# A long convolution's filter spectrum, kept in SBUF for the first group

## The chip, the core and the metric

The kernel runs on one core of a Trainium2 chip. The metric is the device time of one execution in microseconds, the median of several runs. A profile of one execution is at hand beside the times; its engines are PE (TensorE), DVE (VectorE), ACT (ScalarE), POOL (GpSimd) and SP (SyncE, which here only issues transfers).

## What is computed

Two stages, in float32 at the borders. The first is a causal convolution of x (8 batches, 5696 tokens, 128 channels) with a filter h (5696 tokens, 128 channels), by Fourier transforms of twice the length; the second mixes the tokens of its result with two 5696 x 5696 matrices and ends with a small channel product.

```python
L = 2 * S                                  # S = 5696
Y = np.fft.rfft(x, n=L, axis=1) * np.fft.rfft(h, n=L, axis=0)[None]
x = np.fft.irfft(Y, n=L, axis=1)[:, :S, :]
theta = x @ w_theta
zr, zi = x * np.cos(theta), x * np.sin(theta)
u = x + einsum('ts,bsd->btd', w_tok_r, zr) + einsum('ts,bsd->btd', w_tok_i, zi)
out = u + np.maximum(u @ w_ch, 0)
```

## The kernel before

**Groups.** x is worked on in eight groups: four pairs of batches (bp) by two halves of the channels (dh, 64 channels each). The two batches of a pair share one pass as the two halves of the 128 partitions. The transform of length 11392 is split as 178 x 64, and only 90 of the 178 rows (K1 = 90) are needed. A group goes through four stages.

- Stage a (`stage_a`, L241): 16 chunks of four matmuls (L250), each evicted by ACT (L259) or DVE (L257) into a tile `a` of 2 x 90 x 64 float16 columns. The pool that holds `a` has one buffer. The first transform of h goes through the same function and takes that buffer; group 0 has another one (`a_0`), and group 1 takes the buffer of h when h no longer needs it.
- Stage b (`stage_b`, L407): 12 chunks of eight rows (the last has two). 32 small matmuls (`f2`, L262, L270) finish the transform of a chunk, ACT evicts them as `xs` (L426), and DVE multiplies by the spectrum of h and writes `uv_t` (L428; the narrow last chunk L433). A complex product needs the spectrum twice: straight, and with real and imaginary halves swapped. The two halves lie on partitions 0 to 63 and 64 to 127, so a swap moves data across partitions. A tile `hs` (four buffers, `LEAD` = 4) holds both forms of one chunk, and one instruction multiplies by both.
- Stage c (`stage_c`, L439): 16 chunks of sixteen matmuls (L448, L449), evicted by DVE (L455) or ACT (L453) as `g`.
- Stage d (`stage_d`, L473): the last matmuls (L484) and the store of the convolved values.

Stage a of group g+1 is woven into stage c of group g, and stage d of group g into stage b of group g+1.

**The spectrum of h.** `h_chunk` (L351) runs the twelve chunks of `f2` on h, evicts each (DVE L357 or ACT L359) into `hst`, a region of `uv_t` that the products overwrite later, and after every third chunk issues two stores to `hf_hbm` (L364; real and imaginary halves, 384 KB each, eight in all). `hf_hbm` has room for both forms on 128 rows. For group 0 (`first`) two loads per chunk read it back (L416 straight, L417 swapped, 128 KB each, 24 in all). `swap_rows` (L397) then makes the swapped form in HBM by four copies from HBM to HBM (L402, 768 KB each), so that the other seven groups read a chunk with one load (L419).

**Order.** The code around group 0 is: twelve `h_chunk`s with two chunks of stage a between them, the first four chunks' loads, the rest of stage a of group 0, then stage b of group 0, in whose last three chunks three chunks of stage a of group 1 are woven (L541 and L542), then `swap_rows`, then stage c of group 0 woven with the rest of stage a of group 1 and with the making of the tables for stage d (`e_table`, L384). DVE, ACT and POOL keep the order of the code (`manual_schedule`, up to L789). PE and SP do not: a planner orders them by the code's order among what it holds to be ready. Transfers issued by SP go into one hardware queue over the 16 DMA engines; POOL issues the loads of x into another (128-byte pieces, converted to float16 on the way). Nothing on SP is issued before the stores of h.

**The clock.** PE's clock is granted in full or in half. `idle` (L239) and the `warm` matmuls (L276) compute nothing that is used; they keep PE busy.

Lines to have at hand:

```python
        for ri in range(2 if c % 3 == 2 else 0):
            nc.sync.dma_start(hf_hbm[c - 2:c + 1, :, :64, ri, :]..., hst[...])
...
            if first:
                nc.sync.dma_start(hs[:64], hf_hbm[c, dh, :64])
                nc.sync.dma_start(hs[64:], hf_hbm[c, dh, :64, ::-1, :])
            else:
                nc.sync.dma_start(hs, hf_hbm[c, dh])
```

Of the kernel before, what the change touches and what calls it, by code (L numbers as in the profile page):

```python
# [14 lines left out]
mult = mybir.AluOpType.mult  # L15
# [7 lines left out]
def kernel(  # L23
# [10 lines left out]
    nc = tc.nc  # L34
    B, S, D = x.shape
    assert D == 128
    P = 128
# [42 lines left out]
    CK = 8  # L80
    HD = D // 2
# [5 lines left out]
    CHK = [(c0, min(CK, K1 - c0)) for c0 in range(0, K1, CK)]  # L87
    NCK = len(CHK)
# [9 lines left out]
    hf_hbm = nc.dram_tensor("hf_hbm", (NCK, 2, P, 2, HD * CK), F16, kind="Internal").ap()  # L98
# [5 lines left out]
    def psum():  # L104
        return fp.tile([P, 2, 512], F32, tag="ps", name="ps")
# [18 lines left out]
    u_t, v_t = uv_t[:, :UVW + P], uv_t[:, UVW:]  # L124
# [111 lines left out]
    def idle(ps, n, of, m):  # L236

        for i in range(n):
            nc.tensor.matmul(ps[:, i % 2, 512 - m:], of[:, :P], of[:, P:P + m], start=True, stop=True)  # L239

    def stage_a(lhs, by_dve=(), a_=None, spare=None):  # L241

        st = {}

        def chunk(q):
            if q == 0:
                st["a"] = fa.tile([P, 2 * K1, HD], F16, tag="a", name="a_") if a_ is None else a_
            ps = psum()
            for i in range(4):
                nc.tensor.matmul(ps[:, i // 2, (i % 2) * 2 * K1:(i % 2 + 1) * 2 * K1], lhs(q + i), f1_t[:NB],  # L250
                                 start=True, stop=True)
            if spare is not None:
                idle(ps, *spare)
            a_out = st["a"][:, :, q:q + 4].rearrange("p k (a q) -> p k a q", a=2)
            a_in = ps[:, :, :4 * K1].rearrange("p a (q k) -> p k a q", q=2)
            if q // 4 in by_dve:
                nc.vector.tensor_copy(a_out, a_in)  # L257
            else:
                nc.scalar.activation(a_out, a_in, AF.Copy)  # L259
        return [lambda q=q: chunk(q) for q in range(0, HD, 4)], st  # L260

    def f2(a_st, c, warm=WARM):  # L262

        c0, ck = CHK[c]
        ps = psum()
        for j in range(ck):
            for ri in range(2):
                for e in range(2):
                    rows = slice(64 * e, 64 * e + 64)
                    nc.tensor.matmul(ps[:, e, j * HD:(j + 1) * HD],  # L270
                                     w_t2[rows, c0 + j, N2 * (1 - ri):N2 * (3 - ri)],
                                     a_st["a"][rows, ri * K1 + c0 + j, :],
                                     start=(ri == 0), stop=(ri == 1))
        if c == NCK - 1:
            for n in range(warm):
                nc.tensor.matmul(ps[:, n % 2, ck * HD:ck * HD + 384], w_t2[:, 2, :P],  # L276
                                 w_t2[:, 0:2, :].rearrange("p k n -> p (k n)"), start=True, stop=True)
        return ps[:, :, :ck * HD].rearrange("p e (k d) -> p e d k", k=ck)
# [8 lines left out]

    for f in load_x(0):
        f()
    hst = [t[:, :6 * D * CK].rearrange("p (c h d k) -> p c h d k", c=6, h=2, k=CK) for t in (u_t, v_t)]  # L290
    nc.gpsimd.memset(uv_t[:, 2 * UVW:], 0.0)
    k_d = s1.tile([P, 2 * NP + 2 * ND], F32, tag="k_r", name="k_r")
    for at, step, n, base in ((0, 2, NP, 1), (NP, 2, NP, 1), (2 * NP, 2, N2 // 2, 0),
# [40 lines left out]
    def h_copy(d0):  # L334
# [5 lines left out]
    steps, a_h = stage_a(lambda q: h16[:NB].rearrange("p h n d -> p (h n) d")[:, :, q], (1, 3, 5, 9),  # L340
                         spare=(2, pad, 512 - 4 * K1))
    for n, f in enumerate(steps):
# [5 lines left out]
            w2_sine, w2_cosine = w_round(2)  # L348
        f()

    def h_chunk(c):  # L351
        c0, ck = CHK[c]
        ps = f2(a_h, c, 0)
        h_ = hst[c // 6][:, c % 6]
        dst = h_[:, :, :, :ck]
        if c in (0, 2, 5, 7, 10):
            nc.vector.tensor_scalar(dst, ps, 16.0 / NF, None, op0=mult)  # L357
        else:
            nc.scalar.activation(dst, ps, AF.Copy, scale=16.0 / NF)  # L359
        for cc, j in ((0, 0), (NCK - 1, CHK[-1][1] - 1)):  # L360
            if c == cc:
                nc.vector.tensor_scalar(dst[:, :, :, j], dst[:, :, :, j], 0.5, None, op0=mult)
        for ri in range(2 if c % 3 == 2 else 0):
            nc.sync.dma_start(  # L364
                hf_hbm[c - 2:c + 1, :, :64, ri, :].rearrange("c h p n -> p (c h) n"),
                hst[c // 6][64 * ri:64 * ri + 64, c % 6 - 2:c % 6 + 1].rearrange("p c h d k -> p (c h) (d k)"))

    r_u = fc.tile([P, P], F16)
    r_v = fc.tile([P, RC], F16)
# [25 lines left out]
        return curves  # L395

    def swap_rows():  # L397
        for c0 in range(0, NCK, NCK // 2):
            for ri in range(2):
                dst, src = (hf_hbm[c0:c0 + NCK // 2, :, r0:r0 + 64, r, :].rearrange("c h p n -> (c h) p n")  # L400
                            for r0, r in ((64, ri), (0, 1 - ri)))
                nc.sync.dma_start(dst, src)  # L402

# [3 lines left out]
    def stage_b(a_st, dh, warm=WARM, first=False):  # L407

        hs_of = {}

        def load(c):
            if c >= NCK:
                return
            hs = hs_of[c] = fh.tile([P, 2, HD * CK], F16, tag="hs", name="hs")
            if first:
                nc.sync.dma_start(hs[:64], hf_hbm[c, dh, :64])  # L416
                nc.sync.dma_start(hs[64:], hf_hbm[c, dh, :64, ::-1, :])  # L417
            else:
                nc.sync.dma_start(hs, hf_hbm[c, dh])  # L419

        def chunk(c):
            c0, ck = CHK[c]
            hv = hs_of[c].rearrange("p r (d k) -> p r d k", k=CK)
            ps = f2(a_st, c, warm)
            xs = fs.tile([P, 2, HD, CK], F16, tag="xs", name="xs")
            nc.scalar.activation(xs[:, :, :, :ck], ps, AF.Copy)  # L426
            if ck == CK:
                nc.vector.tensor_tensor(  # L428
                    uv[:, :, :, c0:c0 + ck],
                    xs.rearrange("p e d k -> p e (d k)").unsqueeze(1).to_broadcast([P, 2, 2, HD * CK]),  # L430
                    hv.rearrange("p r d k -> p r (d k)").unsqueeze(2).to_broadcast([P, 2, 2, HD * CK]), op=mult)
            for r in range(2 if ck < CK else 0):
                nc.vector.tensor_tensor(  # L433
                    uv[:, 2 * r:2 * r + 2, :, c0:c0 + ck], xs[:, :, :, :ck],
                    hv[:, r:r + 1, :, :ck].to_broadcast([P, 2, HD, ck]), op=mult)
            load(c + LEAD)
        return [lambda c=c: load(c) for c in range(LEAD)], [lambda c=c: chunk(c) for c in range(NCK)]

    def stage_c(st, last):  # L439
# [65 lines left out]
    def front(g, by_dve=(), a_=None, spare=None):  # L505
        if g >= len(groups):
            return [], [], []
        bp, dh = groups[g]
        x16 = x16s[g].rearrange("p b n d -> p (b n) d")
        steps, a_st = stage_a(lambda q: x16[:NB, :, q], by_dve, a_, spare)  # L510
        return (steps, *stage_b(a_st, dh, WARM if g else WARM // 2, g == 0))

    a0, load0, b0 = front(0, (1, 3, 5, 8, 11, 13), a_0, (1, w_t2[:, 2:5].rearrange("p k n -> p (k n)"), 512 - 4 * K1))
    rr = []
    r_rest = [lambda: rr.extend([r_table(0, r_u), r_table(1, r_v)]), lambda: rr[0](), lambda: rr[1]()]
    h_chunk(0)
    w2_sine()
    w_rest(1)
    h_chunk(1)
    w2_cosine()  # L520
    for c in range(2, NCK):
        if c == 5:
            w_rest(2)
        h_chunk(c)
        if c in (9, 10):
            a0.pop(0)()
# [6 lines left out]
    fronts = {1: front(1)}  # L533
    curves = e_table(0)
    for n, f in enumerate(b0):
        f()
        if n == 5:
            curves()
        if n % 2:
            idle(psum(), 1, w_t2[:, 2:6].rearrange("p k n -> p (k n)"), 512)  # L540
        if n > 8:  # L541
            fronts[1][0].pop(0)()  # L542
    setup.close()
    fg = pool("fft_g", 1, conv, side="right")

# [560 lines left out]
    for i, (k, p, tt, j0, s0, nj) in enumerate(stretches):  # L1106
# [22 lines left out]
        a, nxt = nxt, None if i == 1 else prepare(i + 1, not woven)  # L1129
# [15 lines left out]
        if tt is None:  # L1145
# [24 lines left out]
            if end_of_pair:  # L1170
# [5 lines left out]
                c, c0 = c_last  # L1176
# [161 lines left out]
```

## Time and profile before

| what | value |
|---|---|
| median of 3 runs | 2052.54 us (2051.28 to 2053.35) |
| the profiled execution | 2052.18 us, span 2050.4 us |
| mean granted PE clock | 0.987 |
| PE busy, DVE busy, ACT busy, POOL busy | 96%, 75%, 31%, 47% of the span |
| stores of h to HBM (L364) | 8, issued from 30.7 to 44.4 us |
| loads of h for group 0 (L416, L417) | 24, issued from 44.4 to 67.7 us |
| products of group 0 (L428, L433) | from 54.7 to 70.7 us |
| stage c of group 0 | from 70.4 to about 91 us |

How to read it: a row of instruction groups gives line, engine, operation, the tile written and the tiles read, shapes, count, then busy time in all and the mean of one in ns, then how long the engine was idle before them and what ended that. A line of the time line gives start, duration (of all merged instructions), engine and line, and in brackets the idle time before the first one with its releaser. Times count from the span's start. A line of the stretches gives the length, then busy time and instruction count of PE, PE's weight loads, DVE, ACT and POOL, the granted clock, the DMA engines' share and GB/s.

### The profile page before, as it was taken

What the parts mean: (1) busy time and instruction counts of PE and PEld (TensorE: products, weight loads), DVE (VectorE), ACT (ScalarE), POOL (GpSimd) and SP (SyncE); (2) the same over time, 40 slices, a digit from 0 to 9 for tenths busy, and PEclk for the clock granted to TensorE, in tenths of its full rate; (3) what the DMA queues carried; (4) which work ended last, traced back from release to release, by engine and by line L of the source; (5) the groups of instructions that cost most, each with busy time, mean ns of one, the idle gap of its engine ahead of it and who ended that gap; (6) DMA issues with size and microseconds to landing.
All of it is one profiled execution on the core that took longest, in us unless ns stands there. A gap on an engine that the chain in (4) does not pass through costs nothing.

```text
span 2050.4 us, 42565 instructions
## 1 busy us (share of the span) xinstructions
PE 1959.6 (96%) x16205; PEld 1086.2 (53%) x16381; DVE 1538.9 (75%) x2806; ACT 639.9 (31%) x936; POOL 965.2 (47%) x1769
## 2 busy tenths in 40 slices
PE   7799899799999999999999998999999999999998
PEld 5688888654444444444444443444444444444444
DVE  7787777657788888787867667867777686777767
ACT  6788777872232333333300000011111111111111
POOL 8323312384354545454566454453544535354450
PEclk9899999999999999999999999999999999999999
DMA  9999996999899998999999799797887969788793
GB/s 151 187 180 159 146 171 204 238 293 179 163 179 176 170 180 159 179 173 177 170 168 159 119 251 217 107 152 131 150 145 132 155 124 153 131 150 146 131 156 85
DMA packets 510158, 338.21 MB, mean 165 GB/s; under 512 B 184136, under 2 KB 461256, under 8 KB 509864
## 3 DMA queue, kind: packets, MB, share of 16 engines
q0 software_dynamic: 322368, 157.47, 61.0%
q1 hardware_dynamic: 181600, 166.48, 27.8%
q10 hardware_dynamic: 5984, 11.54, 1.6%
q8 instruction: 128, 2.10, 0.4%
q14 instruction: 78, 0.63, 0.1%
HBM read 379.54 MB, written 95.63 MB: 232 GB/s over the span
## 4 chain that ended last, share of the span: by engine, by line
PE 66%; DVE 3%; DMA 2%; issue 1%; POOL 0%; ACT 0%; DVEq 0%; ACTq 0%; SPq 0%
PE m L1275 62%; DMA b<-z_hbm 1%; DVE c L1282 1%; DVE b L831 1%; PE v L977 1%; PE utp L970 1%; PE m L1279 1%; DVE wt L890 1%; PE theta_ps L560 0%; PE tpz L918 0%; PE m L1162 0%; PE m L1196 0%; POOL ring L676 0%; DMA c<-cp_hbm 0%; DMA wl<-in_moe_w_tok_i_dram 0%
## 5 line engine op out<-in xcount | busy, mean ns | idle before, releaser
L676 POOL DMA_DIRECT2D ring<-in_moe_w_tok_i_dram x720 | 387.9, 546 | 657.7 <-DVE wt L890 576.9
L890 DVE STREAM_TRANSPOSE wt<-ring 128x384 f32<-128x384 f32 (+2 forms) x720 | 360.5, 527 | 127.7 <-PE m L1275 77.7
L676 POOL DMA_DIRECT2D ring<-in_moe_w_tok_r_dram x720 | 386.2, 547 | 142.4 <-DVE wt L890 82.4
L1275 PE MATMUL m<-b,wt 128*128 128x512 bf16 x1605 | 386.6, 380 | 3.7 <-DVE wt L890 1.7
L1275 PEld LDWEIGHTS <-wt 128*128 128x128 bf16 x1804 | 176.3, 98 | 219.5 <-DVE wt L890 7.4
L1282 DVE TENSOR_TENSOR c<-c,m 128x512 f32<-128x512 f32 x412 | 266.8, 674 | 0.4 <-PE m L1275 0.4
L972 ACT ACTIVATE ring<-utp 128x512 bf16<-128x512 bf16 x85 | 50.8, 597 | 582.1 <-PE utp L970 582.1
L428 DVE TENSOR_TENSOR uv_t<-xs,hs 128x2048 f16<-128x2048 f16 x88 | 104.4, 1224 | 29.9 <-ACT xs L426 18.2
L448 PE MATMUL ps<-r_u,uv_t 128*128 128x128 f16 x1024 | 116.5, 219 | 4.7 <-ACT cos L588 1.3
L1196 PE MATMUL m<-b,wt 128*128 128x512 bf16 x471 | 110.3, 379 | 7.6 <-DMA b<-z_hbm 4.2
L967 ACT ACTIVATE ub<-c 128x512 bf16<-128x512 f32 x88 | 55.1, 628 | 192.1 <-DVE c L1237 113.5
L449 PE MATMUL ps<-r_v,uv_t 128*128 128x100 f16 x1024 | 114.1, 207 | 0.5
L153 POOL DMA_DIRECT2D x<-in_x_dram x128 | 97.9, 771 | 22.2 <-POOL x L151 14.9
L426 ACT ACTIVATE xs<-ps 128x1024 f16<-128x1024 f32 x96 | 90.8, 972 | 42.4 <-PE ps L270 21.9
L449 PEld LDWEIGHTS <-uv_t 128*128 128x128 f16 x1024 | 99.9, 98 | 7.1 <-issue 5.7
L448 PEld LDWEIGHTS <-uv_t 128*128 128x128 f16 x1024 | 100.0, 98 | 1.1 <-DVE uv_t L433 0.4
L1196 PEld LDWEIGHTS <-wt 128*128 128x128 bf16 x528 | 50.4, 98 | 65.1 <-issue 8.4
L562 ACT ACTIVATE red<-theta_ps,magic 128x512 f32<-128x512 f32 (+1 forms) x46 | 31.6, 687 | 153.1 <-PE theta_ps L560 80.4
L270 PEld LDWEIGHTS <-w_t 64*128 64x128 f16 x3240 | 59.4, 100 | 32.1 <-issue 23.3
L920 ACT ACTIVATE ring<-tpz 128x512 bf16<-128x512 bf16 (+1 forms) x46 | 27.5, 597 | 132.6 <-PE tpz L918 116.3
L250 PE MATMUL ps<-f_t,x 89*128 89x180 f16 x512 | 62.8, 252 | 2.1 <-DVE a L257 1.1
L831 DVE TENSOR_TENSOR b<-b 128x1024 bf16<-128x1024 bf16 x100 | 61.4, 685 | 0.0
(2924 smaller groups left out, 3746.7 us busy)
## 6 DMA issues: line engine op xcount, KB each, us to landing
ring<-in_moe_w_tok_r_dram POOLq DMA_DIRECT2D x352, 96.0 KB, 4.6
ring<-in_moe_w_tok_i_dram POOLq DMA_DIRECT2D x352, 96.0 KB, 4.9
ring<-in_moe_w_tok_r_dram POOLq DMA_DIRECT2D x352, 80.0 KB, 4.5
ring<-in_moe_w_tok_i_dram POOLq DMA_DIRECT2D x352, 80.0 KB, 4.0
cp_hbm<-c SPq DMA_DIRECT2D x88, 256.0 KB, 2.6
c<-cp_hbm SPq DMA_DIRECT2D x88, 256.0 KB, 4.5
out_dram<-c SPq DMA_DIRECT2D x88, 256.0 KB, 4.5
hs<-hf_hbm SPq DMA_DIRECT2D x84, 256.0 KB, 3.4
```

Of the source, the lines that this page charges most:

```text
L153: nc.gpsimd.dma_start(x16[p0:p1, e, n0:n0 + 16, :HD], bass.AP(tensor=src.tensor, offset=src.offset + (p0 * N2 + n0) * D + dh * HD, ap=[[N2 ...
L250: nc.tensor.matmul(ps[:, i // 2, (i % 2) * 2 * K1:(i % 2 + 1) * 2 * K1], lhs(q + i), f1_t[:NB], start=True, stop=True)
L426: nc.scalar.activation(xs[:, :, :, :ck], ps, AF.Copy)
L428: nc.vector.tensor_tensor(uv[:, :, :, c0:c0 + ck], xs.rearrange("p e d k -> p e (d k)").unsqueeze(1).to_broadcast([P, 2, 2, HD * CK]), hv. ...
L448: nc.tensor.matmul(o, u_t[:, at:at + P], r_u, start=True, stop=False)
L449: nc.tensor.matmul(o[:, 2 * NP:], v_t[:, at:at + P], r_v, start=False, stop=True)
L676: nc.gpsimd.dma_start(wb[32 * i:32 * i + 32, :ng, :nj * 64], bass.AP(tensor=a.tensor, offset=a.offset + row0 * S + p * H + i * QR + j0 * 6 ...
L831: return [lambda f=f, x=x: f(*x) for f, x in ((nc.vector.tensor_sub, (bt[M3], b12, b22)), (nc.vector.tensor_sub, (bt[M4], b21, b11)), (nc. ...
L890: nc.vector.transpose(wt.rearrange("p j t r -> p (j t r)").bitcast(F32).rearrange("p (j g t) -> p g j t", j=TJ, g=4)[:, :ng, :nj], wb[:, : ...
L1196: nc.tensor.matmul(ms[n // 2 * 2 + h], a[n][:, j, :, r], bts_of[p][jj][n % 2 * 2 + h][:, r, :], start=(n % 2 == 0 and jj == 0 and r == 0), ...
L1275: nc.tensor.matmul(ms[q], a[q][:, j, :, r], bts[jj][q][:, r, :], start=(jj == 0 and r == 0), stop=(jj == NJ - 1 and r == 1 and q not in left))
L1282: nc.vector.tensor_tensor(c, z, ms[q], op=op)
```

## The change

The evictions of the spectrum of h go into the place of the transform that they were made from (`hst_of`: the tile of h's stage a, two halves of 90 x 64 columns, a chunk at its own rows), not into `uv_t`. They stay there until group 0 has been multiplied. Group 0 reads the straight form there; the swapped form it gets in `hs` by two transfers per chunk within SBUF (64 KB each), lower partitions to upper and upper to lower. A chunk's product is therefore two instructions of half the width, one for each form. The stores to `hf_hbm` are now ten: four after chunk 5 (384 KB each), four after chunk 10 (320 KB each) and two small ones for the last chunk, which has a width of 128 columns in place of 512 in HBM too. `swap_rows` has six copies in place of four: two of 768 KB, two of 640 KB, two of 32 KB. Since the tile of h's transform is in use until the end of stage b of group 0, stage a of group 1 starts after it: three of its chunks leave the last steps of stage b and join the others in stage c.

```diff
-    hst = [t[:, :6 * D * CK].rearrange("p (c h d k) -> p c h d k", c=6, h=2, k=CK) for t in (u_t, v_t)]
...
+    def hst_of(c, n=1):
+        c0 = CHK[c][0]
+        c1 = CHK[c + n - 1][0] + CHK[c + n - 1][1]
+        return a_h["a"].rearrange("p (h k) d -> p h (k d)", h=2)[:, :, c0 * HD:c1 * HD]
...
     def h_chunk(c):
...
-        h_ = hst[c // 6][:, c % 6]
-        dst = h_[:, :, :, :ck]
+        dst = hst_of(c).rearrange("p h (d k) -> p h d k", k=ck)
...
-        for ri in range(2 if c % 3 == 2 else 0):
-            nc.sync.dma_start(
-                hf_hbm[c - 2:c + 1, :, :64, ri, :].rearrange("c h p n -> p (c h) n"),
-                hst[c // 6][64 * ri:64 * ri + 64, c % 6 - 2:c % 6 + 1].rearrange("p c h d k -> p (c h) (d k)"))
+        if c in (NCK // 2 - 1, NCK - 2):
+            n = NCK // 2 if c < NCK // 2 else NCK // 2 - 1
+            for h in range(2):
+                for ri in range(2):
+                    nc.sync.dma_start(hf_hbm[c + 1 - n:c + 1, h, :64, ri, :].rearrange("c p n -> p c n"),
+                                      hst_of(c + 1 - n, n)[64 * ri:64 * ri + 64, h].rearrange("p (c n) -> p c n", c=n))
+        for ri in range(2 if c == NCK - 1 else 0):
+            nc.sync.dma_start(hf_hbm[c, :, :64, ri, :HD * ck].rearrange("h p n -> p h n"),
+                              hst_of(c)[64 * ri:64 * ri + 64])
...
     def swap_rows():
-        for c0 in range(0, NCK, NCK // 2):
+        for c0, c1, w in ((0, NCK // 2, HD * CK), (NCK // 2, NCK - 1, HD * CK), (NCK - 1, NCK, HD * CHK[-1][1])):
             for ri in range(2):
-                dst, src = (hf_hbm[c0:c0 + NCK // 2, :, r0:r0 + 64, r, :].rearrange("c h p n -> (c h) p n")
+                dst, src = (hf_hbm[c0:c1, :, r0:r0 + 64, r, :w].rearrange("c h p n -> (c h) p n")
...
-            if first:
-                nc.sync.dma_start(hs[:64], hf_hbm[c, dh, :64])
-                nc.sync.dma_start(hs[64:], hf_hbm[c, dh, :64, ::-1, :])
-            else:
-                nc.sync.dma_start(hs, hf_hbm[c, dh])
+            w = HD * CHK[c][1]
+            for e in range(2 if first else 0):
+                nc.sync.dma_start(hs[64 * e:64 * e + 64, 1, :w], hst_of(c)[64 - 64 * e:128 - 64 * e, dh])
+            if not first:
+                nc.sync.dma_start(hs[:, :, :w], hf_hbm[c, dh, :, :, :w])
...
-            hv = hs_of[c].rearrange("p r (d k) -> p r d k", k=CK)
+            hv = hs_of[c][:, :, :HD * ck].rearrange("p r (d k) -> p r d k", k=ck)
+            straight = hst_of(c)[:, dh].rearrange("p (d k) -> p d k", k=ck).unsqueeze(1) if first else hv[:, 0:1]
...
-            if ck == CK:
+            if ck == CK and not first:
...
-            for r in range(2 if ck < CK else 0):
+            for r in range(2 if ck < CK or first else 0):
                 nc.vector.tensor_tensor(
                     uv[:, 2 * r:2 * r + 2, :, c0:c0 + ck], xs[:, :, :, :ck],
-                    hv[:, r:r + 1, :, :ck].to_broadcast([P, 2, HD, ck]), op=mult)
+                    (hv[:, 1:2] if r else straight).to_broadcast([P, 2, HD, ck]), op=mult)
...
-        if n > 8:
-            fronts[1][0].pop(0)()
```

## The prediction

> **What bounds the kernel now.** I read the page first (busy shares, then the 40 slices), then the stretches of the first 130 us, then the time line of DVE, ACT and the SP queue between 44 and 70 us. The page says that PE is busy for 96% of the span, and after 350 us no wait of PE has to do with h. The edit lives in the first 90 us only.
>
> ```profile
> PE 1959.6 (96%) x16205; PEld 1086.2 (53%) x16381; DVE 1538.9 (75%) x2806; ACT 639.9 (31%) x936; POOL 965.2 (47%) x1769
> ...
> L428 DVE TENSOR_TENSOR uv_t<-xs,hs 128x2048 f16<-128x2048 f16 x88 | 104.4, 1224 | 29.9 <-ACT xs L426 18.2
> ...
> L831 DVE TENSOR_TENSOR b<-b 128x1024 bf16<-128x1024 bf16 x100 | 61.4, 685 | 0.0
> ```
>
> The reader should keep two prices: a product of 2048 columns shows 1.22 us and takes 104.4/88 = 1.19 back to back; one of 1024 shows 0.685 and takes 61.4/100 = 0.61.
>
> Stretches (PE, PEld, DVE, ACT, POOL busy, granted clock, DMA, GB/s): stage b of group 0 runs from 46 to 70.7, stage c of group 0 to 90.8; the last line is stage c of group 1.
>
> ```profile
> 42.00:52.00 10.00, 9.14 (x190) 7.86 (x190) 6.47 (x12) 5.37 (x7) 5.98 (x8) 0.51 1.54 259
> 52.00:56.00 4.00, 0.83 (x38) 0.64 (x33) 1.31 (x2) 0.00 (x0) 0.00 (x0) 0.93 0.84 202
> 56.00:70.70 14.70, 11.58 (x197) 8.09 (x196) 12.52 (x13) 13.28 (x15) 0.00 (x0) 0.54 0.68 205
> 70.70:90.80 20.10, 18.33 (x355) 17.67 (x355) 19.15 (x19) 17.15 (x23) 12.52 (x21) 1.00 1.33 211
> ...
> 111.90:129.80 17.90, 17.83 (x314) 17.58 (x316) 13.18 (x12) 14.97 (x20) 8.26 (x16) 1.00 1.30 179
> ```
>
> From 52 to 56 every engine nearly stands still; stage c of group 0 has DVE busy for 19.15 of 20.1 us. The time line says what the standstill waits for:
>
> ```profile
> 44.44 1.30 SPq L416 DMA_DIRECT2D hs<-hf_hbm  x1
> ...
> 48.28 1.18 DVE L388 SCALAR_TENSOR_TENSOR e_turns<-e_t,e_turns 90x979 f32<-90x979 f32 x1
> ...
> 49.49 0.67 DVE L198 TENSOR_SCALAR e_t<-e_turns 90x979 uint32<-90x979 uint32 x1
> ...
> 53.73 0.87 SPq L402 DMA_DIRECT2D hf_hbm<-hf_hbm  x1
> 54.69 4.74 DVE L428 TENSOR_TENSOR uv_t<-xs,hs 128x2048 f16<-128x2048 f16 x4 [4.53 <-DMA hs<-hf_hbm]
> ...
> 56.01 2.16 ACT L426 ACTIVATE xs<-ps 128x1024 f16<-128x1024 f32 x2 [6.63 <-DVE uv_t L428]
> ...
> 60.86 1.23 DVE L428 TENSOR_TENSOR uv_t<-xs,hs 128x2048 f16<-128x2048 f16 x1 [1.44 <-DMA hs<-hf_hbm]
> ```
>
> The first product could run at 50.16 (DVE done with L198, xs of chunk 0 ready at 48.5) and runs at 54.69. Its loads were issued by 47.3. The eight stores of the spectrum were issued from 30.7 to 44.4 and each needs 9.7 to 10.2 us to land, so the last lands at about 52.1, and the loads came out right behind: one queue, first in, first out, shared with x loads (q0) that keep the DMA engines full until about 52. A copy (L402) stands in the same queue ahead of the loads of chunk 4, and chunk 4 waits 1.44 us more.
>
> **The change part by part.** 1. Store and read back leave the path of group 0. The unswapped half is read where the eviction put it; the swapped half comes by two SBUF transfers of 64 KB per chunk (24, as before, with half the bytes). They need only the eviction of their chunk, at 28 to 31 us for chunks 0 to 3. The SP queue is ordered by the planner, which fills a waiting queue with later work that is ready: it put the copy at 53.73 ahead of sixteen loads that come before it in the code. SP waits for evictions until 33.4 (chunk 5), so I expect these eight loads ahead of all stores. Then the first product starts at 50.16: **-4.5** (from 0, if they stay behind the stores, to -4.5; DVE's own work excludes more).
>
> 2. Products. Before: 54.69 to 70.70, 16.0 us, with 1.8 of waiting for DMA after the first. After: 22 products of 1024 columns, 22 x 0.61 = 13.5 at least and 22 x 0.685 = 15.1 at most, and 0.7 for the two small ones of the last chunk (L433, 0.40 each, overlapping). ACT's twelve evictions (1.02 each) and two sines (2.2) need 14.4 beside it; PE at half clock 0.95 a chunk and 0.3 for idle matmuls, 15. I take 15.3: **-0.7** (-1.8 to -0.2).
>
> 3. The loads of chunk 4 and on. They leave SP after the product that frees their buffer (51.5), behind whatever the queue holds: the stores (2.9 MB instead of 3.1, but started 2.7 us later, so done at about 51.5 too). The shortest landing of a load is 2.6 us, so 54.5; the swapped product of chunk 4 is due at about 56. With one copy of 768 KB ahead (2.8 us at the 280 GB/s that the queue reached between 70 and 75 us) they are late by 1.3. I take **+0.7** (0 to +2).
>
> 4. Three chunks of stage a of group 1 move from stage b into stage c of group 0, since their tile now holds the spectrum until the last product. In stage b they cost nothing on DVE. In stage c ACT gets 3 x 0.77 = 2.3, less its overlap of 0.08 each: 17.15 + 2.1 = 19.2, as much as DVE's 19.15, in 20.1 us. Stage c of group 1, with all sixteen and no tables, has PE full in 17.9, so PE fits as well. Two engines at 95% that feed one another do not pack: **+1.1** (0, all hidden, to +2.1, none; I stay midway). The first eviction of them now waits on ACT for the last product; behind it stand the sines of the second table and g, and L433 is what PE's L448 waits for anyway, so no further term.
>
> 5. Clock. It is half from 42 to 52.5 and from 56 to 69.6, and full when stage c begins. If stage c starts at half clock, PE's 17.9 us of work stretches for that while. I take **+0.4** (0 to 1.7). The Trainium skill, "TensorE: Matmul & The Clock Gate", Part 1, says that the gate judges free-running windows of about 3.4 us and opens after one busy window; the trace agrees, with steps 3.4 and 13.7 us apart. By that rule stage c could spend a whole window at half clock, 1.7 instead of 0.4, and the sum would be 1.3 us higher; whether it does depends on where 65 us falls in a window, and the edge before 69.6, by the same step, is at 66.2.
>
> 6. At nothing: the evictions of h now write into the transform that they come from; they wait for the same matmuls as before, and writes of interleaved columns by ACT and DVE overlap today in stage a (L257 at 16.57 beside L259 at 17.10). Ten stores instead of eight, and six copies instead of four, cost SP at most 2.0 and 0.9 us each; SP has nothing else until stage b. The loads of group 1 wait behind the copies, as now: they land at 80.2 to 83.1 and are needed at 93.9, a cover of over 10 us. The narrower last chunk saves nothing that is waited for.
>
> Sum: -4.5 - 0.7 + 0.7 + 1.1 + 0.4 = **-3.0 us**. The profiled execution took 2052.18 (span 2050.4 and 1.8 around it), so 2049.2; the median of the runs is 0.36 above, so 2049.5. Later groups and the PE-bound rest pass a shift on.
>
> **The rivals.** A: the loads stay behind the stores, so the change hardly does what it says. For it: they come after the stores in the code, and no load went ahead of a store in the trace (none could: each needed the store). Then the first swapped product starts at 51.5 + 2.6 = 54.1, with the first unswapped one (0.6) already done: -1.2 instead of -4.5, and nothing waits later: -1.2 - 0.7 + 1.1 + 0.4 = -0.4, 2052.1.
>
> B, the slower side: copies HBM to HBM go ahead of the loads of chunk 4. The code has them after stage b, but SP is free between the tenth store (45) and the first freed buffer (51.5), which is longer than before, and one copy already moved up. Each 768 KB costs 2.8 us of queue after 51.5. Two copies: 57.1, landing at 59.5, a wait of 3.5 in place of 0.7, sum -0.2. From the third on it is slower; four make the wait 9 and the sum +5.3, 2057.8. Against it: only one moved up before. By the Trainium skill, "DMA: Bandwidth & Descriptors", Why a DMA increments its semaphore by 16, a copy spreads over the largest number of engines up to 16 that divides its outer size: 12 for the first two, 10 for the next and 2 for the last, 64 packets on each engine in every case. By that rule the smaller copies last as long as the large ones, and all six ahead would cost 16.8 us instead of the 10.4 that their bytes give. The trace has copies of 12 alone, at 8 tenths of the engines.
>
> C: the products lose the double rate. L433 takes 0.40 us for 256 columns, where the slope from 1024 to 2048 (0.53 ns a column) would give 0.28, so short runs can cost. At twice the slope a product of 1024 takes 1.22, and 22 of them 26.8: +11.5 in step 2, sum +9.2, 2061.7. Against: the output already has runs of eight today, at full rate.
>
> **Numbers.** Forecast 0.58, A 0.17, B with three or more copies 0.19, C 0.06. Within the forecast the bounds of steps 2 to 5 add up to -6.3 (-4.5 - 1.8) and +1.1 (-4.5 - 0.2 + 2 + 2.1 + 1.7): 2046.2 to 2053.6, the forecast's own range. With A inside it and B with three and most of four copies, 2046.0 to 2057.5 leaves out C, B with all six, and a little below. 0.2% is 4.1 us, about what a measurement of this kernel can tell from no change: faster has 0.23, the part of the forecast under 2048.4; slower is B, all but three copies (0.17), and C (0.06): 0.23; the rest, with A, is 0.54.
>
> **What would show it.** Step 1: loads of hs on SP before the first store, and the first unswapped product at about 50. Step 2: 22 products at 0.6 to 0.7 us. Step 3: waits of DVE for hs at chunk 4, and the place of the L402 copies on SP. Step 4: stage c of group 0 in 21 to 22 us. Step 5: the clock of its first 3.4 us. The prediction falls if the copies crowd the queue, or if the planner orders SP and PE anew further down, which no view of before can show.

## The result, and the profile after

The changed kernel takes 2066.51 us (median of six runs, 2063.17 to 2073.48); the kernel before, in the same comparison, 2051.6 (six runs, 2045.5 to 2053.35). The ratio is 1.0078, with a 95% interval of 1.0063 to 1.0093: the change costs about 15 us. The forecast was 2049.5, a gain of 3, with a range to 2057.5; the sign is wrong and the time lies outside the range.

The profiled execution took 2067.78 us, with a span of 2066.0 and a mean granted clock of 0.984 (before: 0.987). From the page of the changed kernel, the line of the busy times:

```profile
PE 1958.2 (95%) x16205; PEld 1085.0 (53%) x16381; DVE 1537.5 (74%) x2817; ACT 639.1 (31%) x936; POOL 964.7 (47%) x1769
```

PE's busy time is 1.4 us less than before, DVE's 1.4 and ACT's 0.8 less, and the span is 15.6 us longer. The work has not grown; the time is idle time. The same stretches as before (PE, PEld, DVE, ACT, POOL busy, granted clock, DMA, GB/s) show where, except that the first now begins at 30:

```profile
30.00:42.00 12.00, 3.64 (x141) 3.51 (x133) 2.66 (x4) 1.23 (x2) 11.19 (x15) 0.65 1.71 196
42.00:52.00 10.00, 3.87 (x56) 3.17 (x56) 3.20 (x3) 3.52 (x4) 2.96 (x5) 0.50 1.07 181
52.00:56.00 4.00, 1.53 (x11) 1.37 (x10) 0.07 (x1) 0.00 (x0) 0.00 (x0) 0.50 0.83 193
56.00:70.70 14.70, 10.20 (x156) 9.52 (x157) 8.73 (x21) 8.75 (x14) 0.00 (x0) 0.60 0.32 96
70.70:90.80 20.10, 13.18 (x336) 10.83 (x329) 18.41 (x29) 16.12 (x18) 0.26 (x2) 0.85 0.42 111
```

From 30 to 56 us PE is busy for 9.04 of 26 us, DVE for 5.93 and ACT for 4.75, and the products of stage b, which began at 54.69 before, fill the stretch from 70.70 on. The time line of the changed kernel between 24 and 87 us (start, time, engine, line, operation, and in brackets the idle time ahead of it and what ended it) tells what was waited for:

```profile
27.75 5.11 SPq L425 DMA_DIRECT2D hs<-a__241  x8
...
33.00 6.85 SPq L370 DMA_DIRECT2D hf_hbm<-a__241  x4
...
43.94 0.87 SPq L410 DMA_DIRECT2D hf_hbm<-hf_hbm  x1
...
47.05 2.86 ACT L362 ACTIVATE a__241<-ps 128x1024 f16<-128x1024 f32 x3 [15.83 <-DMA hf_hbm<-a__241]
47.08 1.23 DVE L360 TENSOR_SCALAR a__241<-ps 128x1024 f16<-128x1024 f32 x1 [14.30 <-DMA hf_hbm<-a__241]
48.13 0.76 PE L250 MATMUL ps<-f_t,x 89*128 89x180 f16 x4 [14.20 <-ACT a__241 L362]
...
51.32 3.94 SPq L370 DMA_DIRECT2D hf_hbm<-a__241  x4
...
58.81 0.38 ACT L362 ACTIVATE a__241<-ps 128x256 f16<-128x256 f32 x1 [8.24 <-DMA hf_hbm<-a__241]
...
59.23 0.24 DVE L365 TENSOR_SCALAR a__241<-a__241 128x128 f16<-128x128 f16 x1 [7.16 <-ACT a__241 L362]
59.25 0.76 PE L250 MATMUL ps<-f_t,x 89*128 89x180 f16 x4 [5.71 <-ACT a__241 L362]
...
70.54 0.69 DVE L442 TENSOR_TENSOR uv_t<-xs,a__241 128x1024 f16<-128x1024 f16 x1 [0.62 <-ACT xs L435]
...
86.17 0.29 PE L457 MATMUL ps<-r_u,uv_t 128*128 128x128 f16 x1 [2.11 <-DVE uv_t L442]
```

The forecast looked for trouble at the loads. The loads are in order: eight of hs (L425) leave SP at 27.75, ahead of the first store (L370) at 33.00, as step 1 said. What waits is the eviction of h into `a__241`. The first four stores, which read chunks 0 to 5, are issued from 33.00 on; ACT (L362) and DVE (L360) then stand for 15.83 and 14.30 us before they write chunk 6 and the next, PE finds no free accumulator (`ps`, which the evictions empty) and stands for 14.20, and all go on as the stores have landed. After the second group of four (51.32) the eviction of the last chunk waits 8.24 in the same way. The list of waits of the changed kernel from 24 to 75 us (who, for whom: us in total, times, longest) adds it up:

```profile
ACT a__241 L362 <- DMA hf_hbm<-a__241: 24.1, 2, 15.8
...
PE ps L250 <- ACT a__241 L362: 19.9, 2, 14.2
DVE a__241 L360 <- DMA hf_hbm<-a__241: 14.3, 1, 14.3
```

In the same list of the kernel before, the evictions of h (there into `uv_t`) wait for their matmuls alone:

```profile
ACT uv_t L359 <- PE ps L270: 2.3, 4, 1.2
...
DVE uv_t L357 <- PE ps L270: 1.6, 2, 0.9
```

In the changed kernel PE stops for 19.9 us in two waits. The first product runs at 70.54 instead of 54.69, stage c of group 0 starts at 86.2 instead of 70.4 (+15.8) and ends at 107.6 instead of 90.1. The two stops less the 4.5 that step 1 of the forecast was to gain would give 15.4, an estimate close to the 15.85 by which the first product is late. At the end of stage c the lag is 17.5, and the span is 15.6 us longer, so about 2 us are made up further on; where, was not followed.

The granted clock explains little of this. From 42 to 52 it is half in both kernels (0.50 and 0.51); it is lower than before from 30 to 42 (0.65 for 1.00) and from 52 to 56 (0.50 for 0.93), in stretches in which PE is busy for less than half of the time.

### The profile page after: what moved, and what is told of

It is laid out like the page before. It is cut to its first block, busy times and chain, and to the rows that moved or that the text cites. A ratio compares the mean times of both kernels' runs of the same rounds, so it can differ in the third digit from the quotient of the medians.

```text
span 2066.0 us, 42583 instructions
## 1 busy us (share of the span) xinstructions
PE 1958.2 (95%) x16205; PEld 1085.0 (53%) x16381; DVE 1537.5 (74%) x2817; ACT 639.1 (31%) x936; POOL 964.7 (47%) x1769
## 4 chain that ended last, share of the span: by engine, by line
PE 65%; DMA 3%; DVE 3%; issue 1%; POOL 1%; ACT 0%; ACTq 0%; DVEq 0%; SPq 0%
PE m L1282 61%; DMA ring<-in_moe_w_tok_r_dram 1%; DVE c L1289 1%; PE v L984 1%; PE utp L977 1%; DMA b<-z_hbm 1%; PE m L1286 1%; DVE b L838 1%; DVE wt L897 1%; POOL ring L683 1%; DMA ring<-in_moe_w_tok_i_dram 0%; PE theta_ps L567 0%; PE tpz L925 0%; PE m L1203 0%; DMA zl<-zl_hbm 0%
## 5 line engine op out<-in xcount | busy, mean ns | idle before, releaser
L437 DVE TENSOR_TENSOR uv_t<-xs,hs 128x2048 f16<-128x2048 f16 x77 | 91.5, 1223 | 18.1 <-ACT xs L435 12.0
L435 ACT ACTIVATE xs<-ps 128x1024 f16<-128x1024 f32 x96 | 90.8, 972 | 30.9 <-PE ps L270 15.6
L250 PE MATMUL ps<-f_t,x 89*128 89x180 f16 x512 | 66.2, 262 | 21.2 <-ACT a__241 L362 19.9
L270 PEld LDWEIGHTS <-w_t 64*128 64x128 f16 x3240 | 55.3, 97 | 27.1 <-issue 19.8
L250 PEld LDWEIGHTS <-x 89*128 89x128 f16 x512 | 51.3, 158 | 22.4 <-issue 22.0
```

What stands on the lines that cost most here:

```text
L270: nc.tensor.matmul(ps[:, e, j * HD:(j + 1) * HD], w_t2[rows, c0 + j, N2 * (1 - ri):N2 * (3 - ri)], a_st["a"][rows, ri * K1 + c0 + j, :], s ...
L437: nc.vector.tensor_tensor(uv[:, :, :, c0:c0 + ck], xs.rearrange("p e d k -> p e (d k)").unsqueeze(1).to_broadcast([P, 2, 2, HD * CK]), hv. ...
```

## The experiments

The puzzle is that the waiting evictions touch no byte that the stores read: the stores read chunks 0 to 5, the evictions write chunk 6 and on. In columns of the tile, chunk c has 512 in the lower channel half, from 512c on, and 512 in the upper half, from 5760 + 512c on (5760 is 90 x 64). An eviction writes both runs in one instruction. My theory, S: the order between a transfer and such a write is kept by spans. The eviction of chunk 6 writes 3072 to 3584 and 8832 to 9344; taken as one span, 3072 to 9344, it covers what the store of the upper half of chunks 0 to 5 reads (5760 to 8832), and not what that of the lower half reads (0 to 3072). The rivals: T, that any store that reads the tile holds every later write to it; and the prediction's rival B, that copies in the queue are what is late. Against B the time line above speaks already: two copies (L410, at 43.94 and 55.35) go ahead of the loads of chunk 4, and no product (L442) waits for a transfer. Against T speaks the kernel before: its first two stores of h leave SP at 30.71 and take 9.7 us or more to land, and evictions into other columns of the same tile run until 36.6 without a wait for them. There each chunk lies in one stretch of `uv_t` of its own. The first kernel only asks whether the waits are all of the loss.

No kernel here leaves anything of the computation out. Comparisons are made within one group of runs, since the median of the kernel before differed between groups (2051.6, 2048.02, 2049.14).

### All stores behind the last eviction

```diff
-        if c in (NCK // 2 - 1, NCK - 2):
-            (four stores)
+        if c == NCK - 1:
+            for c_ in (NCK // 2 - 1, NCK - 2):
+                h_store(c_, (0, 1))      # the same four stores
+            h_store_last()               # the two of the last chunk
```

> All ten stores of the spectrum are issued after the last eviction of h; nothing else differs from the changed kernel. Theory S (an eviction of chunk 6 or later waits for earlier stores of the upper channel half, because the two runs that it writes, 5760 columns apart, are taken as one span and those stores lie inside it): no eviction waits for a store, the stops of PE of 14.2 us and 5.7 us go, the last eviction of h is at 37 to 39 us as before the change, the first product of group 0 near 50, and the rest of the recorded sum holds: about 2048.6 us, 2 to 4 under before. Theory T (any store in flight from the tile blocks every write to it): the same, since no write follows. Theory K (the stops are a consequence of the half clock or of full DMA engines and not of a wait that the kernel contains): DMA engines are as full, so stops of about 10 us or more stay, 2060 or above.

Measured: 2045.21 us (ten runs) against 2048.02 before (13 runs), ratio 0.9983 (0.9968 to 0.9999). So the waits of the evictions are the whole loss, and what is left is the forecast gain, 2.8 us where 3.0 was forecast. Theory K falls: the DMA engines are as full from 30 to 42 us (a share of 1.81, in the changed kernel 1.71), and no wait of PE is longer than 2.3 us. The time line of this kernel on DVE between 30 and 90 us:

```profile
37.54 0.66 DVE L365 TENSOR_SCALAR a__241<-a__241 128x128 f16<-128x128 f16 x1
...
48.68 0.68 DVE L450 TENSOR_TENSOR uv_t<-xs,a__241 128x1024 f16<-128x1024 f16 x1
49.28 0.69 DVE L450 TENSOR_TENSOR uv_t<-xs,hs 128x1024 f16<-128x1024 f16 x1
...
57.05 0.69 DVE L450 TENSOR_TENSOR uv_t<-xs,hs 128x1024 f16<-128x1024 f16 x1 [2.75 <-DMA hs<-a__241]
...
65.35 0.39 DVE L450 TENSOR_TENSOR uv_t<-xs,hs 128x256 f16<-128x256 f16 x1
```

The last eviction is done before 37.54 (in the changed kernel at 59.2), the first product runs at 48.68, right after L198 on DVE, and of the products only one, in chunk 4, waits for a transfer, 2.75 us. The SP queue from 44 to 60 us shows one copy ahead of the loads of that chunk; whether it is the cause is tried further down.

```profile
49.78 0.91 SPq L418 DMA_DIRECT2D hf_hbm<-hf_hbm  x1
50.79 9.27 SPq L433 DMA_DIRECT2D hs<-a__241  x11
```

### Which half's stores do it

Only the stores of one channel half stay where the change has them; those of the other go behind the last eviction. S says that the upper half alone stops the evictions; T says that either does.

```diff
         if c in (NCK // 2 - 1, NCK - 2):
-            (stores of halves 0 and 1)
+            h_store(c, (0,))             # the other kernel: (1,)
+        if c == NCK - 1:
+            for c_ in (NCK // 2 - 1, NCK - 2):
+                h_store(c_, (1,))        # the other kernel: (0,)
```

> The four stores of the lower channel half (chunks 0 to 5 and 6 to 10) are issued where the changed kernel issues them; those of the upper half after the last eviction. Theory S: the span of an eviction of chunk 6 begins behind the lower half's chunks 0 to 5, so no eviction waits: about as the kernel with all stores last, 2047 to 2051 us. Theory T: the evictions wait for the two lower stores, the stop is about 10 us and the time 2058 or above.

> The mirror image: the stores of the upper channel half stay where the changed kernel has them, those of the lower half come after the last eviction. Theory S: the evictions of chunk 6 wait as in the changed kernel, but behind two stores instead of four, so the stop is shorter by the time of two stores: 8 to 11 us instead of 14.2, and again some us at chunk 11; 2056 to 2064 us. Theory T: the same. With the run before, only S expects the two to differ.

Measured, one execution each: with the lower half early 2045.96 us (stage c of group 0 starts at 65.9), with the upper half early 2065.42 (80.2). Each lies 1.0 to 1.4 us outside the range that S gave; the 19.5 us between them are what is read here, since the kernel before alone ran from 2044.95 to 2052.21 in this group. In the list of waits from 24 to 75 us of the kernel with the upper half's stores early, the two stops are back:

```profile
ACT a__241 L362 <- DMA hf_hbm<-a__241: 17.8, 2, 11.6
...
PE ps L250 <- ACT a__241 L362: 14.2, 2, 10.4
DVE a__241 L360 <- DMA hf_hbm<-a__241: 10.1, 1, 10.1
```

In the same list of the kernel with the lower half's stores early the evictions wait for their matmuls alone:

```profile
ACT a__241 L362 <- PE ps L270: 2.8, 4, 1.1
DVE uv_t L452 <- DMA hs<-a__241: 2.7, 1, 2.7
DVE a__241 L360 <- PE ps L270: 2.7, 2, 1.6
```

T falls: the lower stores read the same tile at the same time, with the same bytes, and hold nothing. The waits with the upper half alone are shorter (10.1 instead of 14.3 on DVE), which fits two stores in the queue instead of four.

### The stores where they were, each eviction in two

If S holds, an eviction with one instruction per channel half writes one run at a time, no span covers what a store reads, and the stores may stay where the change has them.

```diff
-        nc.vector.tensor_scalar(dst, ps, 16.0 / NF, None, op0=mult)    # or nc.scalar.activation
+        for e in range(2):
+            nc.vector.tensor_scalar(dst[:, e], ps[:, e], 16.0 / NF, None, op0=mult)   # or the same on ACT
```

(The halving of a column by L365 is cut in the same way.)

> The stores stay where the changed kernel has them; each eviction of h is two instructions, one for each channel half, so that each writes one unbroken run. Theory S: no wait for stores. Twelve evictions in two halves cost DVE and ACT some 0.2 us each more, at most 2 us on the way to the stores' end, and stage b starts near 51: 2048 to 2053 us. Theory T: the stops stay, 2064 or above.

> The same kernel as the one with evictions by halves, timed in rounds. Theory S predicted 2048 to 2053 us and one look gave 2043.6 us; I expect a ratio of 0.996 to 0.999 against before, the gain of 3 us that the recorded sum has once no eviction waits, give or take 2 us.

Measured: 2043.59 us in a single execution, and 2045.67 as the median of ten, ratio 0.9978 (0.9962 to 0.9995). That is less than the 2048 to 2053 expected, in part because a pair of halves takes 1.29 us on DVE and 1.09 on ACT where the whole took 1.22 and 1.02, so cutting costs 0.07 us and not 0.2. In the list of waits of the single execution, no eviction waits for a transfer; what ACT's wait for is this:

```profile
ACT a__241 L363 <- PE ps L270: 2.7, 4, 1.3
```

The bytes written, the bytes stored and the place of the stores are those of the changed kernel; only the form of the write differs, and some 20 us of PE's waits are gone. This and the two kernels before it show S from outside: order, half and form of the write each decide as the spans say. How the planner builds its waits I have not seen; that it takes the two runs as one span is inferred from these runs. Engine against engine it does not seem to: in the changed kernel PE's matmuls (L270, x120 in one run, from 28.95) read later columns of the same tile while DVE and ACT write earlier ones, and the only wait of theirs is one for the table w_t.

### The copies behind the loads

What is left to lose is the wait of 2.75 us at chunk 4. Here the copies of group 0 may only be issued after the last SBUF transfer of group 0.

```diff
+                first_load["last"] = nc.sync.dma_start(hs[...], hst_of(c)[...]).ins
...
-                nc.sync.dma_start(dst, src)
+                with tc.issue_after(first_load["last"]):
+                    nc.sync.dma_start(dst, src)
```

> The kernel with all stores last, and the copies within HBM tied behind the last transfer of the swapped form of group 0 on SP. In the kernel with all stores last one copy of 768 KB stands ahead of the transfers of chunk 4, and DVE waits 2.75 us for them. If that copy is what they wait behind (theory C), the wait goes or falls under 0.5 us, stage c of group 0 starts at 62.5 to 63.5 instead of 65.5, and the time falls by 2 to 3 us against the kernel with all stores last: a ratio of 0.9965 to 0.998 against before, if that one is at 0.998. If the transfers wait behind the ten stores (theory D), the wait stays at 2 to 3 us and the time is that of all stores last.

> Evictions in two halves, the stores where the changed kernel has them, and the copies behind the transfers of group 0. Theory C and D agree that there is no wait at chunk 4 here, since the stores start earlier and there is none in the kernel with split evictions: about the same as that one, ratio 0.996 to 0.9985 against before; stage c of group 0 starts at 65.5 to 66.5.

> The kernel before, with only the copies tied behind the loads of group 0. It has one copy ahead of the loads of chunk 4 and waits 1.44 us there. Theory C: that wait shrinks and the kernel is 1 to 2 us faster than before, ratio 0.999 to 0.9995, so the edit of the spectrum is not needed for this part of the gain. Theory D: no change.

Measured: with the stores last 2044.37 us (twelve runs), ratio 0.9976 (0.9962 to 0.999); with the evictions cut 2045.92 (twelve runs), 0.9981 (0.9967 to 0.9996), and stage c of group 0 starting at 65.2, just ahead of the range given; the kernel before with this edit alone 2050.66 (ten runs), 1.0009 (0.9994 to 1.0024). The before of these groups is 2049.14. In the time line of the first, on DVE from 44 to 70 us, no product of chunk 4 waits for a transfer (its swapped one runs at 54.17); one of chunk 5 does for 0.21 us, and the next waits for ACT:

```profile
54.17 0.69 DVE L454 TENSOR_TENSOR uv_t<-xs,hs 128x1024 f16<-128x1024 f16 x1
...
55.67 0.69 DVE L454 TENSOR_TENSOR uv_t<-xs,hs 128x1024 f16<-128x1024 f16 x1 [0.21 <-DMA hs<-a__241]
57.68 0.69 DVE L454 TENSOR_TENSOR uv_t<-xs,a__241 128x1024 f16<-128x1024 f16 x1 [1.31 <-ACT xs L447]
```

So theory C is right on the wait, and D is not: the same ten stores are in the queue. But of the 2.75 us, 0.21 and 1.31 came back as the two waits shown, and stage c of group 0 starts at 64.3 instead of 65.5, not at the 62.5 to 63.5 that C gave. The kernels with evictions in two agree as far as they go: a copy leaves SP 3.7 and 4.1 us ahead of the loads of chunk 4 there, not 1.0, and no product waits for a transfer, with the copies ahead or behind. The medians of the two kernels with and without this edit differ by less than their intervals, so the edit's own worth is not settled; with the stores last it has the lowest ratio measured. The intervals of all four mended kernels that were run ten times or more lie below 1. In the kernel before with the same edit, the time line on DVE reads:

```profile
53.59 1.23 DVE L431 TENSOR_TENSOR uv_t<-xs,hs 128x2048 f16<-128x2048 f16 x1 [4.03 <-DMA hs<-hf_hbm]
...
58.73 1.23 DVE L431 TENSOR_TENSOR uv_t<-xs,hs 128x2048 f16<-128x2048 f16 x1 [0.16 <-DMA hs<-hf_hbm]
```

The 4.03 us for the read-back stay, the wait at chunk 4 shrinks from 1.44 to 0.16, and stage c still starts at 70.6 (before 70.4): the 1 to 2 us that C gave this kernel did not come. So the gain of the mended kernels comes from keeping the spectrum in SBUF, not from the copies.

## Why the prediction was wrong

The step that failed is step 6, in the words "At nothing: the evictions of h now write into the transform that they come from; they wait for the same matmuls as before". They wait for stores too: 15.83 and 8.24 us on ACT, 14.30 on DVE, 19.9 in all on PE, against a price of nothing with no second end. The row put beside it, L257 at 16.57 next to L259 at 17.10, is of two engines that write one tile; it says nothing on a transfer that reads the tile while an engine writes it. That pair is new in this form with the change. Before, stores and evictions shared `uv_t` too, and the evictions did not wait; but each chunk lay there in one stretch of its own, and no row of the trace of before has a transfer reading between two runs of a later write. It was an operation that the trace did not show, and so it wanted a bound on both sides. The rows for it were there: a store needs 9.7 to 10.2 us to land, and the change has two groups of four with evictions still to come behind each, which makes a loss of 20 us from two waits for a group. No rival had this mechanism. (Two readings in the same step are too low, without weight in the result: a store holds SP for up to 2.24 us, not 2.0, and a copy for up to 1.75, not 0.9.)

The other steps are read from the kernel with the stores last, where no eviction waits for a transfer:

- **Step 1** (-4.5): held, and was worth more. The loads go ahead of the stores, and the first product runs at 48.68 (forecast 50.16, before 54.69): -6.0. DVE reached the end of L198 1.4 us earlier; why is not shown. The profiles of the other mended kernels have the first product at 48.6 to 51.3, so the size of this step is known to some 2.7 us only. Rival A is false.
- **Step 2** (-0.7): the 24 products take 17.06 us from 48.68 to 65.74, of which 2.75 is the wait of step 3, so 14.3, where 15.3 was forecast. A product of 1024 columns shows 0.69 and comes every 0.60. Rival C is false.
- **Step 3** (+0.7, bound 2): mis-sized; 2.75. The place was right, chunk 4, and so was the cause that the text named, one copy ahead of the loads. The landing was right as well: 54.5 + 2.8 makes 57.3, and the wait ended at 57.05. (The sum in the text has a slip: 51.5 + 2.6 is 54.1, which makes 56.9, and late by 0.9 instead of 1.3.) What was off is when the product is due: at 54.30 instead of about 56, since the products began 1.5 us earlier than forecast and came faster. What steps 1 and 2 gained beyond the forecast ran into this wait. Rival B in its priced form, three or more copies, did not come: one is ahead, in this kernel. The number of DMA engines that smaller copies use was tried by no run.
- **Step 4** (+1.1): stage c of group 0 takes 21.1 us instead of 19.7, +1.4. From its stretch:

```profile
65.50:86.60 21.10, 18.78 (x316) 17.84 (x318) 18.93 (x19) 18.89 (x24) 11.64 (x19) 1.00 1.22 195
```

  ACT has 18.89 us of work in it, DVE 18.93 and PE 18.78: three engines at 89 to 90% that do not pack closer.
- **Step 5** (+0.4): nothing. The granted clock in that stretch is 1.00. In the kernel with the stores last and the copies behind, stage c has a part at half clock inside it:

```profile
65.40:68.80 3.40, 3.15 (x31) 2.94 (x30) 3.37 (x4) 2.80 (x4) 0.18 (x1) 0.50 0.83 286
```

  The mean is 0.92 over 21.0 us, and 0.08 x 21.0 / 0.5 = 3.4 us. Stage c is no longer for it (21.1 us in both kernels). With evictions in two and a clock of 0.88, 5.1 us at half, it takes 21.4, 0.3 more. The 3.4 us agree with the windows of about 3.4 us of the Trainium skill, "TensorE: Matmul & The Clock Gate", Part 1; the price of 1.7 us that a whole window would have by that rule did not show. The other half of the rule as the prediction put it, that one busy window opens the gate, the trace of before does not bear out: PE is busy, as the profile counts it, for 3.39 of the 3.41 us from 42.12, and the next 3.42 us are still granted at 0.50.

Together: -6.0 at the first product, then 16.8 instead of 15.7 us until stage c starts (48.68 to 65.5, before 54.69 to 70.4), +1.1, and +1.4 in stage c: -3.5 in one execution, beside -2.8 in the medians and the forecast -3.0. The sum came out right for a kernel whose evictions do not wait, but not its terms: steps 1 and 2 gained 1.5 and 1.0 more than forecast, and steps 3 and 4 lost 2.05 and 0.3 more, step 5 0.4 less. The first three are in good part one thing, since products that are due sooner wait longer for the same transfer; the rest of the agreement is luck. The kernel at hand was another one.

## What to carry to other kernels

When a tile gets a second use, list for every pair of old and new accesses that now share it (transfer and engine as well as engine and engine) whether one can be held for the other, and price the pair at the landing time of the transfer until a row of the same form shows that it overlaps. A write of two runs far apart may be held as if it wrote all that lies between; one instruction per run, or stores behind the last write, took away 20 us of PE's waits here, and both kernels came out about 0.2% faster than the one before (0.9978 and 0.9983). A chain of small, well-priced terms is worth little beside one unpriced "at nothing".

## What was not expected of the hardware

One copy of 768 KB within HBM, issued 1.0 us ahead of loads of 64 KB, made a product wait: the loads of chunk 4 were issued from 50.79, and the product that needs them ran at 57.05, 6.3 us later. Without the copy they were issued from 49.95 and were there by 54.17, at most 4.2 us later; with a copy 3.7 to 4.1 us ahead, no product waited.

And two halves of the same stores, of equal bytes, were worth 2045.96 and 2065.42 us by the columns that they read alone. As far as these runs show, that is the order that the program was given, and not the chip's doing.
